# Spacing the search rounds of a routed expert layer by round, behind matmuls that set the clock

## The chip, the cores and the metric

One core of one Trainium2 chip runs the kernel. The metric is device microseconds from one execution, so smaller is better. TensorE is called PE below and its weight loads PEld; VectorE is DVE, ScalarE is ACT, GpSimd is POOL, and SP is the engine that issues most DMAs.

## The reference

Attention over 8 batches with 8 heads of 576 rows and 64 columns: half of the heads see a band of 32 keys, half see every 32nd key. Its output, as 4608 rows of 512, is routed to 8 experts of at most 576 rows each, and every expert is two matrix products with a ReLU between them. Rows are given out greedily over all scores in falling order:

```python
logits = x @ w_gate
order = np.argsort(-logits.flatten())
for idx in order:
    tok, e = idx // E, idx % E
    if assigned[tok] >= 0 or counts[e] >= cap:
        continue
    assigned[tok] = e
    counts[e] += 1
for e in range(E):
    mask = assigned == e
    out[mask] = np.maximum(x[mask] @ w1[e], 0.0) @ w2[e]
```

## The kernel before

**Two stages.** The attention stage fills some 236 us. It leaves the rows in DRAM (`x_scr`) and the scores `L` in SBUF. The expert stage follows, and the change touches it alone.

**Experts in the order in which they fill.** The kernel doesn't sort. It finds which expert is full first, and at which score; it gives that expert its rows, closes it, points the other rows to their next best expert, and searches for the next one to fill. The expert that fills first is phase 0, the last one is phase 7. Each phase runs one expert: a first layer (192 matmuls of 288 columns, L1167, in eight blocks of 24), then a second layer (96 of 512 columns, L1215, and 24 half-height ones, L1209). After each block of the first layer ACT writes the ReLU `hh` (L1174) and DVE the remainder `hl` (L1175), since every product is made from f16 halves.

**A search** (`search`) has seven rounds, 0 to 6. A round cuts an interval of scores in 18. DVE compares all rows with 17 candidates (`cm`, L811). PE counts (nine matmuls, L827), DVE folds the counts (`red` L830, `r` L833), PE sums them (L836), DVE compares them with the capacity (`g`, L843, or L840 in round 6), PE adds that up (L846), and DVE makes the next candidates (`cand`, L849). Then `settle` and `number` name the expert, `weights` starts its weight loads, `slots` (L899 on PE) numbers its rows, `indices` turns the numbers into a list of rows (L955 and L963 on PE, `idx` on DVE L967), and `tokens` gathers the rows on POOL (L1072, five gathers `xr`). `halve` splits them into f16 halves on ACT and DVE (`xg`, L1061 and L1062) and transposes them by DMA into `xt` (L1063). `xt` and the halved weights are what the next phase needs. The weights take squares on ACT (`jk`, L994), a scale (L1000, L1002 on PE, L208), and a halving on ACT (L1012) and DVE (L1013), sixteen pieces in all.

**What sets the order.** PE's order is the order in which the program is written out, and everything there waits in that order. `ffn` yields a cost after each matmul (123 for 288 columns, 216 for 512), and a clock in the program adds these up. Each chain of side work (search, list, weights) is a generator: it yields the number of units after which its next step is written out, and a step's matmuls land on PE at that point between the expert's own. So the yields of `search` are the spacing between a step's work on DVE and the matmul that consumes it, in units of about one ns of PE's own work. The other engines' order comes from the scheduler of the framework, which takes the steps by priority (`urgent`) and by its own estimate of times; on the chip each engine then works through its list in order. `side` runs the searches one behind the other, and the search for expert `ph` may not end before phase `ph - 2` is written out. Once phase `ph` begins, the steps of its weights that are left are written out at once (`rush`).

**What the steps of the prediction touch.** `pace` in `search` gives the units of a step: 2950 before the counts, 1350 before the sum, 1225 before the step (`T_COUNT`, `T_SUM`, `T_STEP`), and 0.55 of them while only one expert is closed, which is the search for expert 1. `T_HOT` (4200) stands between the comparisons of the list and L955, with `T_HOT1` (6350) for expert 1.

Of the kernel before, what the change touches and what calls it, by code (L numbers as in the profile page):

```python
# [19 lines left out]
N, DM, E, FF = B * S, H * D, 8, 1024  # L20
# [28 lines left out]
URGENT = 4000  # L49
T_FIRST, T_COUNT, T_SUM, T_STEP, T_PREFIX, T_NEXT, T_HOT, T_DUP, T_LOAD = 1100, 2950, 1350, 1225, 3900, 2300, 4200, 550, 8000  # L50
PACE1 = 0.55
H0 = 256
HURRY = (0, 1, 7)
MAN, MAN0, MANP = {mybir.EngineType.PE}, {mybir.EngineType.Activation}, (0,)
T_W20, T_STEP0 = 9000, 1000
X1 = 100
# [3 lines left out]
T_F, T_LOAD0, T_HOT1, T_W, T_SQ, T_SCALE, T_CUT, T_BULK0 = 3000, 1500, 6350, 4000, 1500, 1500, 1500, 600  # L60
# [77 lines left out]
def band_stride_attention_then_capacity_moe(ctx, tc, qt, kl, ks, nl, ns, wg, w1, w2, cst, out, dbg=None):  # L138
# [81 lines left out]
    with tc.tile_pool(name="ld", bufs=2) as ld, \  # L220
# [20 lines left out]
        for g in "sl":  # L241
            for i in range(2):
                t = ld.tile([128, 32], F32, name=f"mx_{g}{i}", bufs=1)
                nc.gpsimd.memset(t, 0.0)
                mxb[g, i] = t
                t = ld.tile([128, ST if g == "s" else LT, 4, VW], F32, name=f"v_{g}{i}", bufs=1)
# [481 lines left out]
    scat, closed, first, second = [], [], [], []  # L728
    ready, emitted, rush = set(), set(), set()

    def urgent(ph=1):
        return tc.high_priority(offset=URGENT * (2 if ph == 0 else 1))
# [12 lines left out]
    def settle(hp, top, w):  # L745
        mm = rt.tile([TP, 1], F32, name="mm")
        nc.vector.tensor_reduce(mm, hp, axis=AX.X, op=OP.max)
        w8 = rt.tile([TP, E], F32, name="w8")
        nc.vector.scalar_tensor_tensor(w8, hp, mm, desc8, op0=OP.is_equal, op1=OP.mult)
        mv = rt.tile([TP, 1], F32, name="mv")  # L750
        nc.vector.scalar_tensor_tensor(mv, mm, -1.0, w, op0=OP.add, op1=OP.mult)
        nc.vector.tensor_tensor(mv, mv, top, op=OP.add)
        return mv, w8
# [43 lines left out]
                    nc.tensor.matmul(pm[:, :E], ones_j[:J], g, start=True, stop=True)  # L797
                    return settle(pm[:, :E], top, grid[:, rd, J0:])

    def pace(t):  # L800
        return t if len(closed) > 1 else t * PACE1

    def search(rm, ohc, more):
        cand, src, top = cand0, rm, None
        ohv = ohc.rearrange("p c e -> p (c e)")
        for rd in range(R1):
            last = rd == R1 - 1
            t = cand[:, :J1] if last else cand[:, 1:J1 + 1]
            with urgent():
                cm = rt.tile([TP, NC, J1], F16, name="cm")  # L810
                nc.vector.tensor_tensor(cm, src[:, :, None].to_broadcast([TP, NC, J1]),  # L811
                                        t[:, None, :].to_broadcast([TP, NC, J1]), op=OP.is_ge)
                cv = cm.rearrange("p c j -> p (c j)")
                n = 1 if rd == R1 - 2 else J1 + 1
                if not last:
                    pre = cand[:, 0:1]
                    if n > 1:
                        pre = rt.tile([128, n], F32, name="pre1")
                        nc.vector.tensor_scalar(pre, steps[:, rd + 1, :n], cand[:, 0:1], None, op0=OP.add)
                if rd == 0:  # L820
                    more()
            yield pace(T_COUNT) + (X1 if len(closed) == 1 else T_FIRST if rd == 0 else 0)
            with urgent():
                pr = ps_r.tile([128, 512], F32, name="pr_")
                pc, p2, pm = pr[:GC * J1, :GC * E], pr[:, 64:64 + E], pr[:, 128:128 + (E if last else 1)]
                for k in range(0, NC, GC):
                    nc.tensor.matmul(pc, cv[:, k * J1:(k + GC) * J1], ohv[:, k * E:(k + GC) * E], start=(k == 0),  # L827
                                     stop=(k == NC - GC))
                red = rt.tile([GC * J1, GC, E], F16, name="red")
                nc.vector.tensor_tensor(red.rearrange("p c e -> p (c e)"), pc, fold[:, :GC * E], op=OP.mult)  # L830
                r8 = rt.tile([GC * J1, E], F16, name="r8")
                with nc.allow_low_precision(reason="whole numbers up to 1152"):
                    nc.vector.tensor_reduce(r8, red.rearrange("p c e -> p e c"), axis=AX.X, op=OP.add)  # L833
            yield pace(T_SUM)
            with urgent():
                nc.tensor.matmul(p2, fold[:, GC * E:], r8, start=True, stop=True, skip_group_check=True)  # L836
                g = rt.tile([128, E], F16, name="g1")
                ih = rt.tile([128, 1], F16, name="ih1")
                if last:
                    nc.vector.tensor_scalar(g, p2, float(CAP), None, op0=OP.is_ge)  # L840
                else:
                    with nc.allow_low_precision(reason="zero or one"):
                        nc.vector.tensor_scalar(g, p2, float(CAP), 0.0, op0=OP.is_ge, op1=OP.max, accum_out=ih)  # L843
            yield pace(T_STEP)
            with urgent():
                nc.tensor.matmul(pm, ones_j, g if last else ih, start=True, stop=True, skip_group_check=True)  # L846
                if not last:
                    cand = rt.tile([128, n], F32, name=f"cand{n}")
                    nc.vector.scalar_tensor_tensor(cand, steps[:, rd, J1 + 1:].to_broadcast([128, n]), pm, pre,  # L849
                                                   op0=OP.mult, op1=OP.add)  # L850
                if rd == R1 - 2:
                    top, src = cand, rt.tile([TP, NC], F32, name="rml")
                    nc.vector.tensor_scalar(src, rm, top, None, op0=OP.subtract)
                    cand = steps[:, rd + 1, :J1 + 1]
        with urgent():
            return settle(pm, top, steps[:, R1 - 1, J1 + 1:])
# [72 lines left out]
    def indices(ph, slot):  # L929
        hurry = ph in HURRY  # L930
        with urgent(ph) if hurry else nullcontext():
            si = rt.tile([TP, 2, NC], I32, name="si")
            nc.vector.tensor_copy(si[:, 0], slot)
            nc.vector.tensor_single_scalar(si[:, 1], si[:, 0], SLO - 1, op=OP.bitwise_and)
            nc.vector.tensor_single_scalar(si[:, 0], si[:, 0], 6, op=OP.logical_shift_right)
            sh = rt.tile([TP, 2, NC], F16, name="sh")
            nc.vector.tensor_copy(sh, si)
            ohh = rt.tile([TP, SHI, NC], F16, name="ohh")
            nc.vector.tensor_tensor(ohh, sh[:, 0:1].to_broadcast([TP, SHI, NC]), iota[:, :SHI], op=OP.is_equal)
            rv = rvb[ph % 2]  # L940
            nc.vector.tensor_tensor(rv[:, :3 * SHI].rearrange("p (h a) c -> p h a c", a=3), ohh[:, :, None].to_broadcast([TP, SHI, 3, NC]),
                                    val[:, None].to_broadcast([TP, SHI, 3, NC]), op=OP.mult)
            nh = NC // 3
            ohl = []
            for h in range(3):
                o = r1.tile([TP, SLO, nh], F16, name=f"ohl{h}")
                nc.vector.tensor_tensor(o, sh[:, 1:2, h * nh:h * nh + nh].to_broadcast([TP, SLO, nh]),
                                        iota[:, :, :nh], op=OP.is_equal)
                ohl.append(o)
        yield T_HOT1 if ph == 1 else T_HOT  # L950
        with urgent(ph):
            pi = ps_r.tile([128, 512], F32, name="pr_")
            for c in range(NC):
                g = c % 4
                nc.tensor.matmul(pi[HV * g:HV * g + HV, :SLO], rv[:, :, c], ohl[c // nh][:, :, c % nh], start=(c < 4),  # L955
                                 stop=(c >= NC - 4), skip_group_check=True)
            p1 = rt.tile([128, SLO], F16, name="p1")
            nc.vector.tensor_copy(p1, pi[:, :SLO])
        yield T_DUP
        with urgent(ph):  # L960
            p2 = ps_r.tile([128, 512], F32, name="pr_")
            for u in range(2):
                nc.tensor.matmul(p2[SLO * u:SLO * u + SLO, :2 * NT], p1, pick[:, u], start=True, stop=True,  # L963
                                 skip_group_check=True)
            idx = rt.tile([128, 2, NT], I32, name="idx", bufs=3)
            nc.vector.tensor_copy(idx.rearrange("p a t -> p (a t)"), p2[:, :2 * NT])
            nc.vector.tensor_single_scalar(idx[:, 1], idx[:, 1], 23, op=OP.logical_shift_left)  # L967
        return idx[:, 0], idx[:, 1].bitcast(F32)
# [208 lines left out]
    def ffn(ph, wts, xt, idx, sx):  # L1177
# [5 lines left out]
        if ph == 0:  # L1183
            t0 = H0 // 128
            for f in first[TURN_E:t0]:
                f()
            for c in (slice(0, H0), slice(H0, CAP)):
                for f in range(FC):
# [150 lines left out]
```

## Time and profile before

| | us |
|---|---|
| median of three runs | 696.55 |
| lowest, highest | 696.18, 700.16 |
| the profiled execution | 693.16 |
| its span, first to last instruction | 691.4 |
| PE busy in the span | 615.7 (89%) |
| DVE busy | 460.1 (67%) |
| ACT busy | 330.6 (48%) |
| POOL busy | 111.5 (16%) |
| mean granted clock of PE | 0.947 |

All times in the text are positions in the profiled execution's span, which ends 1.76 us short of that execution's time. In the rows, a bracket at the end is how long the engine had stood idle before that instruction, and what ended this. A busy PE means little here, since a matmul's duration overlaps the next one's; the distance from one start to the next, and the waits, say what a phase costs.

### The profile page before, as it was taken

To read this page: it belongs to the slowest core of one execution; us is meant where nothing else is said; L and a number is where in the kernel's file an instruction comes from. 1 tells how busy PE (TensorE), PEld (TensorE's weight loads), DVE (VectorE), ACT (ScalarE), POOL (GpSimd) and SP (SyncE) were. 2 spreads that over 40 slices of the span, in tenths; PEclk is the share of its full clock that TensorE was granted. 3 is DMA by queue.
4 is the path that set the end of the run, shared out by engine and by line. 5 is a ranking of instruction groups with operands and counts; after the bars stand their busy time and mean duration, and the time that the engine had idled before them with its cause. 6 is when DMAs were issued, how large, how long until landed. Compare 5 with 4: busy or idle time off the path is not lost.

```text
span 691.4 us, 19758 instructions
## 1 busy us (share of the span) xinstructions
PE 615.7 (89%) x8294; PEld 404.1 (58%) x8298; DVE 460.1 (67%) x1389; ACT 330.6 (48%) x551; POOL 111.5 (16%) x124
## 2 busy tenths in 40 slices
PE   8789998999964789989989979989999998999993
PEld 4567776766743465457448537547646744745741
DVE  4857776787857879786776777777778656580200
ACT  2443643464410644772762564484385277771210
POOL 2100110111000200410340140051042041211011
PEclk9898998999965899999999999999999998999997
DMA  8996888795210821860870770590293188731010
GB/s 233 250 256 176 249 234 212 212 265 162 68 41 2 271 65 35 306 109 1 298 153 1 264 172 16 177 241 33 105 270 78 60 276 236 221 59 50 1 39 31
DMA packets 76364, 102.42 MB, mean 148 GB/s; under 512 B 41292, under 2 KB 49062, under 8 KB 75763
## 3 DMA queue, kind: packets, MB, share of 16 engines
q1 hardware_dynamic: 68195, 79.61, 40.9%
q0 software_dynamic: 7360, 21.15, 9.9%
q8 instruction: 65, 1.06, 0.7%
q10 hardware_dynamic: 720, 0.39, 0.2%
q14 instruction: 24, 0.20, 0.1%
HBM read 73.60 MB, written 18.87 MB: 134 GB/s over the span
## 4 chain that ended last, share of the span: by engine, by line
PE 23%; issue 13%; DVE 10%; DMA 10%; POOL 4%; ACT 3%; SPq 1%; POOLq 0%; DVEq 0%; ACTq 0%
PE ph L1167 16%; DMA w<-in_w_dram 4%; DMA xr<-x_scr,idx 4%; PE ph L1215 3%; POOL xr L1072 3%; DVE w1l L1013 2%; DMA xt<-xg 2%; DVE w2l L1013 2%; POOL out_dram L1226 1%; DVE xg L1062 1%; DVE cm L811 1%; ACT jk L994 1%; PE ph L1209 1%; DVE hl L1175 1%; ACT xg L1061 1%
## 5 line engine op out<-in xcount | busy, mean ns | idle before, releaser
L1167 PE MATMUL ph<-xt,w1h 128*128 128x288 f16 (+2 forms) x1024 | 177.9, 289 | 6.4 <-DMA xt<-xg 4.1
L1167 PEld LDWEIGHTS <-w1h 128*128 128x128 f16 x1024 | 97.6, 99 | 37.8 <-issue 7.7
L1167 PE MATMUL ph<-xt,w1l 128*128 128x288 f16 (+2 forms) x512 | 111.7, 289 | 0.0
L1226 POOL DMA_INDIRECT out_dram<-y,idx x40 | 49.6, 1239 | 332.5 <-ACT y L1225 304.4
L1215 PE MATMUL ph<-w2h,hh 128*128 128x512 f16 x256 | 97.0, 379 | 0.8 <-DVE hl L1175 0.8
L1215 PE MATMUL ph<-w2h,hl 128*128 128x512 f16 x256 | 97.0, 379 | 0.0
L1215 PE MATMUL ph<-w2l,hh 128*128 128x512 f16 x256 | 97.0, 379 | 0.0
L994 ACT ACTIVATE jk<-w 128x1024 f16<-128x1024 f32 x64 | 67.4, 1054 | 61.6 <-DMA w<-in_w_dram 60.6
L1174 ACT ACTIVATE hh<-ph 128x576 f16<-128x576 f32 (+2 forms) x72 | 42.6, 593 | 110.8 <-PE ph L1167 110.6
L1215 PEld LDWEIGHTS <-hh 128*128 128x128 f16 x512 | 49.1, 98 | 58.2 <-issue 7.8
L1175 DVE SCALAR_TENSOR_TENSOR hl<-ph,hh 128x576 f16<-128x576 f32 (+2 forms) x72 | 49.5, 687 | 47.4 <-ACT hh L1174 47.3
L1167 PEld LDWEIGHTS <-w1l 128*128 128x128 f16 x512 | 50.5, 99 | 14.1 <-issue 1.3
L373 ACT ACTIVATE pr<-spa 128x576 f32<-128x576 f32 x32 | 20.8, 650 | 72.0 <-PE spa L370 50.3
L1072 POOL DMA_INDIRECT xr<-x_scr,idx x40 | 41.8, 1045 | 53.3 <-DVE L L920 25.3
L1013 DVE SCALAR_TENSOR_TENSOR w1l<-w,w_sw,w1h 128x512 f16<-128x512 f32 x64 | 45.5, 744 | 4.7 <-ACT w1h L1012 4.5
L1215 PEld LDWEIGHTS <-hl 128*128 128x128 f16 x256 | 24.9, 97 | 39.3 <-issue 14.3
L1013 DVE SCALAR_TENSOR_TENSOR w2l<-w,w_sw,w2h 128x512 f16<-128x512 f32 x64 | 46.4, 744 | 1.8 <-ACT w2h L1012 1.6
L1012 ACT ACTIVATE w2h<-w,w_sw 128x512 f16<-128x512 f32 x64 | 41.2, 710 | 6.0 <-DVE w_sw L208 6.0
L1012 ACT ACTIVATE w1h<-w,w_sw 128x512 f16<-128x512 f32 x64 | 42.4, 708 | 3.2 <-DVE w_sw L208 2.1
L1225 ACT ACTIVATE y<-ph,so 128x512 f32<-128x512 f32 x32 | 21.7, 679 | 43.9 <-PE ph L1215 31.6
L424 POOL DMA_DIRECT2D x_scr<-xs x23 | 15.3, 670 | 168.0 <-DVE xs L408 125.2
L1062 DVE TENSOR_TENSOR xg<-xr,xg 128x512 f16<-128x512 f32 (+1 forms) x37 | 25.3, 687 | 18.5 <-ACT xg L1061 18.3
(603 smaller groups left out, 951.5 us busy)
## 6 DMA issues: line engine op xcount, KB each, us to landing
w<-in_w_dram SPq DMA_DIRECT2D x64, 512.0 KB
kl<-in_kl_dram SPq DMA_DIRECT2D x16, 304.0 KB
v_s<-in_ns_dram SPq DMA_DIRECT2D x16, 292.5 KB
v_l<-in_nl_dram SPq DMA_DIRECT2D x16, 292.5 KB
ks<-in_ks_dram SPq DMA_DIRECT2D x16, 288.0 KB
qs<-in_qt_dram SPq DMA_DIRECT2D x16, 288.0 KB
ql<-in_qt_dram SPq DMA_DIRECT2D x16, 288.0 KB
x_scr<-xl SPq DMA_DIRECT2D x8, 512.0 KB
```

The costliest lines, as they stand in the source:

```text
L373: nc.scalar.activation(pr[:, :S].rearrange("k (h n) -> k h n", h=2), u.sp[p][:, :, :HS], AF.Exp, scale=0.125)
L994: nc.scalar.activation(jk, wf[:, c * n4:(c + 1) * n4].rearrange("p c f -> p (c f)"), AF.Square, scale=1.41422, accum_out=sq[:, c:c + 1])
L1012: nc.scalar.activation(hi[:, c, f], wf[:, c, f], AF.Copy, scale=s_)
L1013: nc.vector.scalar_tensor_tensor(lo[:, c, f], wf[:, c, f], s_, hi[:, c, f], op0=OP.mult, op1=OP.subtract)
L1062: nc.vector.tensor_tensor(xs[:, 1], xv, xs[:, 0], op=OP.subtract)
L1072: nc.gpsimd.indirect_dma_start(out=xr[:n], out_offset=None, in_=x_rows, in_offset=bass.IndirectOffsetOnAxis(ap=idx[:n, t:t + 1], axis=0))
L1167: nc.tensor.matmul(tile_[:, j, :w], wt[:, d, f * 128:(f + 1) * 128], xt[:, d // 2, xx, d % 2, c], start=(k == 0), stop=(k == 3 * DC - 1))
L1174: nc.scalar.activation(hv, src, AF.Relu)
L1175: nc.vector.scalar_tensor_tensor(lv, src, 0.0, hv, op0=OP.max, op1=OP.subtract)
L1215: nc.tensor.matmul(py, a[:, f, ts_], w[:, f], start=(k == 0), stop=(k == len(todo) - 1))
L1225: nc.scalar.activation(y, py, AF.Copy, scale=so[:, t:t + 1])
L1226: st = nc.gpsimd.indirect_dma_start(out=out_rows, out_offset=bass.IndirectOffsetOnAxis(ap=idx[:n, t:t + 1], axis=0), in_=y[:n], in_offset= ...
```

## The change

Three numbers. In the searches for experts 2 to 6 (two or more experts closed), rounds 4, 5 and 6 have all three distances cut to 0.72: 2124, 972 and 882 units. In rounds 1 and 2 the distance between the counts (L827) and the sum (L836) grows by 1000, from 1350 to 2350. In the list of the last expert, the distance before L955 grows from 4200 to 6350. No instruction is added or taken away. A search is written out over 3 x 1547 - 2000 = 2641 units fewer, and since the searches follow one another, each later one starts earlier within its phase. Lines behind 51 have a number higher by one in the kernel after.

```diff
+PACE, CROWDED, T_MORE = (1, 1, 1, 1, 0.72, 0.72, 0.72), (1, 2), 1000
...
-    def pace(t):
-        return t if len(closed) > 1 else t * PACE1
+    def pace(t, rd):
+        return t * PACE[rd] if len(closed) > 1 else t * PACE1
...
-            yield pace(T_COUNT) + (X1 if len(closed) == 1 else T_FIRST if rd == 0 else 0)
+            yield pace(T_COUNT, rd) + (X1 if len(closed) == 1 else T_FIRST if rd == 0 else 0)
...
-            yield pace(T_SUM)
+            yield pace(T_SUM, rd) + (T_MORE if len(closed) > 1 and rd in CROWDED else 0)
...
-            yield pace(T_STEP)
+            yield pace(T_STEP, rd)
...
-        yield T_HOT1 if ph == 1 else T_HOT
+        yield T_HOT1 if ph in (1, E - 1) else T_HOT
```

DVE in phase 3, round 1 of the search for expert 5. `pr__7439` (before) and `pr__7396` (after) are the same PSUM tile of counts, `xg` are the halves of expert 4's gathered rows, `y` is output of the running phase. Before:

```order
L1062 TENSOR_TENSOR xg<-xr,xg 128x2x256
L830 TENSOR_TENSOR red<-pr__7439,fold 68x32
L1062 TENSOR_TENSOR xg<-xr,xg 128x2x256
L833 TENSOR_REDUCE r_7451<-red 68x8
L1062 TENSOR_TENSOR xg<-xr,xg 128x2x256
L843 TENSOR_SCALAR g_7467,ih_7468<-pr__7439 128x8
L1062 TENSOR_TENSOR xg<-xr,xg 128x2x256
```

After:

```order
L1063 TENSOR_TENSOR xg<-xr,xg 128x2x256
L831 TENSOR_TENSOR red<-pr__7396,fold 68x32
L1063 TENSOR_TENSOR xg<-xr,xg 128x2x256
L834 TENSOR_REDUCE r_7408<-red 68x8
L1063 TENSOR_TENSOR xg<-xr,xg 128x2x256
L1224 SCALAR_TENSOR_TENSOR y<-ph,so,yl 64x512
L1063 TENSOR_TENSOR xg<-xr,xg 128x2x256
L844 TENSOR_SCALAR g_7437,ih_7438<-pr__7396 128x8
```

The fourth `xg` and the output piece `y` have moved ahead of `g`, which PE's L846 (L847 after) consumes; the fold `r` stands behind two `xg` as it did.

PE in phase 5, the second part of the list for expert 6 (`p` and `pick` belong to the list, `w1l` to the first layer, `w2l`, `w2h`, `hh` and `hl` to the second). Before:

```order
L1215 MATMUL ph<-w2l,hh 128x512
L963 LDWEIGHTS p_8889
L963 MATMUL pr__8903<-pick,p_8889 64x10
L963 LDWEIGHTS p_8889
L963 MATMUL pr__8903<-pick,p_8889 64x10
L1215 LDWEIGHTS hl
L1215 MATMUL ph<-w2h,hl 128x512
```

After:

```order
L1168 MATMUL ph<-xt,w1l 128x288
L964 LDWEIGHTS p_8806
L964 MATMUL pr__8813<-pick,p_8806 64x10
L964 LDWEIGHTS p_8806
L964 MATMUL pr__8813<-pick,p_8806 64x10
L1168 LDWEIGHTS w1l
L1168 MATMUL ph<-xt,w1l 128x288
```

The list has moved from the second layer (behind 59 of its 120 matmuls) into the first layer (behind 185 of 192).

ACT in phase 5, around the end of the first layer: `jk` are squares of expert 6's weights, which wait for their loads. Before:

```order
L1174 ACTIVATE hh<-ph 128x576 x7
L994 ACTIVATE jk,sq<-w_8684 128x1024 x2
L1225 ACTIVATE y<-ph,so 128x512
L994 ACTIVATE jk,sq<-w_8684 128x1024 x2
L1222 ACTIVATE yl<-ph,so 64x512
```

After:

```order
L1175 ACTIVATE hh<-ph 128x576 x5
L995 ACTIVATE jk,sq<-w_8583 128x1024 x2
L1175 ACTIVATE hh<-ph 128x576
L995 ACTIVATE jk,sq<-w_8583 128x1024 x2
L1175 ACTIVATE hh<-ph 128x576
L995 ACTIVATE jk,sq<-w_8592 128x1024 x3
L1175 ACTIVATE hh<-ph 128x576
```

The squares now stand between the `hh` of the first layer, where they stood behind all of them.

## Prediction

> **What bounds the kernel now.** I read the table of stretches first, one stretch per phase of the expert stage. Its columns are busy time by engine (with counts), then the granted clock and the DMA share.
>
> ```profile
> 357.70:413.70 56.00, 51.96 (x433) 32.99 (x432) 40.94 (x128) 30.12 (x50) 12.36 (x10) 1.00 0.48 139
> 404.60:409.00 4.40, 4.18 (x22) 1.94 (x22) 3.72 (x12) 4.08 (x8) 0.00 (x0) 1.00 1.15 229
> 523.30:575.30 52.00, 50.79 (x401) 31.90 (x399) 35.22 (x118) 28.84 (x49) 9.13 (x10) 1.00 0.47 144
> 575.30:578.50 3.20, 0.26 (x1) 0.04 (x1) 2.91 (x9) 2.33 (x4) 1.58 (x2) 0.86 0.62 149
> 578.50:584.70 6.20, 6.16 (x27) 3.95 (x28) 3.40 (x5) 3.02 (x6) 0.00 (x0) 0.52 0.98 367
> 632.90:680.10 47.20, 47.20 (x313) 29.29 (x311) 6.80 (x9) 8.63 (x13) 4.78 (x5) 1.00 0.07 26
> ```
>
> The bare phase 7 takes 47.2 us at full clock: that is what PE needs for one expert. Phase 2 takes 56.0. So PE bounds the stage, and what can be won is PE's waits and its slow clock. Second, the list of PE's waits in this stage (total, times, longest):
>
> ```profile
> PE ph L1167 <- DMA xt<-xg: 4.1, 2, 3.0
> PE pr__6674 L836 <- DVE r L833: 2.8, 1, 2.8
> PE pr__7519 L836 <- DVE r L833: 1.8, 1, 1.8
> PE pr__5989 L836 <- DVE r L833: 1.7, 1, 1.7
> PE pr__9204 L955 <- DVE rv L941: 1.4, 1, 1.4
> PE pr__8284 L836 <- DVE r L833: 1.3, 1, 1.3
> PE pr__6754 L836 <- DVE r L833: 1.0, 1, 1.0
> PE pr__8204 L836 <- DVE r L833: 0.9, 1, 0.9
> PE pr__5142 L836 <- DVE r L833: 0.8, 1, 0.8
> PE pr__8903 L963 <- DVE p L958: 0.7, 1, 0.7
> PE pr__5909 L836 <- DVE r L833: 0.6, 1, 0.6
> PE pr__7439 L836 <- DVE r L833: 0.5, 1, 0.5
> PE pr__7628 L836 <- DVE r L833: 0.3, 1, 0.3
> ```
>
> The tiles 5909, 6674, 7439 and 8204 are round 1 of the searches for experts 3 to 6, and 5989, 6754, 7519 and 8284 their round 2. So the added 1000 units stand where PE waits most. Round 1 sums to 0.6 + 2.8 + 0.5 + 0.9 = 4.8 us, round 2 to 1.7 + 1.0 + 1.8 + 1.3 = 5.8.
>
> **Rounds 1 and 2, the first edit.** One such wait in phase 2, on DVE and in order:
>
> ```profile
> 396.03 0.17 DVE L967 TENSOR_SCALAR idx<-idx 128x5 int32<-128x5 int32 x1
> 401.84 0.18 DVE L830 TENSOR_TENSOR red<-pr__6674,fold 68x32 f16<-68x32 f32 x1
> 403.96 0.69 DVE L1062 TENSOR_TENSOR xg<-xr,xg 128x512 f16<-128x512 f32 x1 [1.93 <-ACT xg L1061]
> 404.57 0.20 DVE L833 TENSOR_REDUCE r<-red 68x8 f16<-68x32 f16 x1
> 406.13 0.69 DVE L1062 TENSOR_TENSOR xg<-xr,xg 128x512 f16<-128x512 f32 x1 [0.68 <-ACT xg L1061]
> ```
>
> DVE isn't short of time: it stands 1.93 us before the second `xg`, whose gathered rows aren't there yet, and the fold `r` (0.20 us) is queued behind it. 1000 units become four matmuls of 512 columns, 4 x 0.216 = 0.86 us. But the gathers start from `idx`, and the whole search moves with the list, so their distance to round 1 stays, and the new order puts up to four `xg` ahead of `g`. From phase 4:
>
> ```profile
> 507.19 0.17 DVE L967 TENSOR_SCALAR idx<-idx 128x5 int32<-128x5 int32 x1
> 513.81 0.20 DVE L833 TENSOR_REDUCE r<-red 68x8 f16<-68x32 f16 x1
> 515.71 0.69 DVE L1062 TENSOR_TENSOR xg<-xr,xg 128x512 f16<-128x512 f32 x1 [0.62 <-ACT xg L1061]
> ```
>
> PE reached that L836 at 514.0 - 0.9 = 513.1, 5.9 after `idx`; now it gets there at 6.8, and at L846 six matmuls (1.3 us) later, at 8.1. The fourth `xg` ends 515.71 + 0.69 - 507.19 = 9.2 after `idx` here, 10.8 in phase 2. With `g` behind it, PE waits 1.1 to 2.7 at L846 instead. By the order, `g` stands behind the fourth `xg` in three searches (in the first of them behind a weight piece too) and behind the third in the search for expert 4. I take 1.9, 0.3, 1.3 and 0.5 = 4.0, and 0.8 left at L836: as much as the 4.8 before. **Round 1 comes to 0**, bounded by a gain of 4.8 if the gathers land sooner and a loss of some 6 if each is as late as in phase 2 (4 x 2.7 - 4.8). In round 2, the last `xg` and most weight pieces now stand ahead of `cm`, and the four extra matmuls come on top: I leave 0.9 of 5.8, **-4.9**, between -5.8 and -3.4 (0.86 won at each of four, less than that nowhere). The 0.8 of tile 5142 is in phase 0. What it wins is waited for again at phase 1's first matmuls, where 4.1 - 3.0 = 1.1 us go to `xt`, whose gathers and transposes don't move: 0.
>
> **Rounds 4 to 6, the second edit.** Round 6 in phase 2, in the first layer:
>
> ```profile
> 378.49 0.45 PE L827 MATMUL pr__6324<-ohn,cm 128*68 128x32 f16 x9
> 379.19 0.20 DVE L833 TENSOR_REDUCE r<-red 68x8 f16<-68x32 f16 x1
> 380.13 0.17 PE L836 MATMUL pr__6324<-r,fold 68*128 68x8 f16 x1
> 380.36 0.17 DVE L840 TENSOR_SCALAR g<-pr__6324 128x8 f16<-128x8 f32 x1 [0.97 <-PE pr__6324 L836]
> 381.16 0.76 DVE L1175 SCALAR_TENSOR_TENSOR hl<-ph,hh 128x576 f16<-128x576 f32 x1 [0.63 <-ACT hh L1174]
> 381.38 0.17 PE L846 MATMUL pr__6324<-g,ones_j 128*128 128x8 f16 x1
> ```
>
> `r` is ready 0.74 us before its matmul (380.13 - 379.39) and `g` 0.85 (381.38 - 380.53). The cut takes away three and two matmuls of 0.123, so 0.37 and 0.60 are left. In itself the second edit is free; nothing is cheaper either, since no work goes. An `hl` in between (0.76) now costs up to 0.4 at `r`. More costly is where rounds 3 and 4 come to lie: at a phase's start, among the second weight's pieces.
>
> ```profile
> L1013 DVE SCALAR_TENSOR_TENSOR w2l<-w,w_sw,w2h 128x512 f16<-128x512 f32 x64 | 46.4, 744 | 1.8 <-ACT w2h L1012 1.6
> ```
>
> One piece of 0.744 us between `red` and `r` exceeds the 0.37 by 0.4. Round 3 already paid 0.3 there (tile 7628). For four searches, two rounds, one such piece each I take 8 x 0.4 - 3 x 0.3 = **+2.3**, between 0 and +5.
>
> **What the drift moves.** The searches get 2641 units shorter, so by phase 5 the list for expert 6 is written out 7 matmuls of 0.123, 24 + 11 of 0.216 and 24 of 0.109 sooner: 0.9 + 7.6 + 2.6 = 11 us. At the start of phase 6 stands the largest stall of the stage:
>
> ```profile
> 561.89 0.17 DVE L967 TENSOR_SCALAR idx<-idx 128x5 int32<-128x5 int32 x1
> 578.54 0.90 PE L1167 MATMUL ph<-xt,w1h 128*128 128x288 f16 x3 [2.98 <-DMA xt<-xg]
> 597.85 1.06 ACT L994 ACTIVATE jk<-w 128x1024 f16<-128x1024 f32 x1 [2.78 <-DMA w<-in_w_dram]
> 600.19 0.63 ACT L1174 ACTIVATE hh<-ph 128x576 f16<-128x576 f32 x1
> ```
>
> `xt` was complete 16.7 us after its `idx` (578.54 - 561.89), 3 us too late; 11 us sooner, it is there 8 us early. That saves the 2.98, and the half clock behind it: 6.20 us at 0.52 is a loss of 6.20 x 0.48 = 2.98. **-6.0**, at least -3 should the clock fall elsewhere. On the clock, the 2.8 us wait of phase 2 left it at 1.00 (404.60 to 409.00), the 3.2 us stretch brought it to 0.52. [...]
>
> The list itself now lies in the first layer in phases 4 and 5 (and at its end in phase 3). There its steps on DVE share the queue with `hl`, which waits for `hh`, which on ACT now stands behind squares that wait for weight loads, as in phase 6 before: a square stood 2.78 us, and the `hh` behind it came at 600.19. PE has three PSUM buffers in `ph`, which covers a late `hh`; what isn't covered is L955 and L963 of the list. I take one `hl` (0.76) in phases 4 and 5, half in phase 3, less the 0.7 of tile 8903: **+1.2**, between -0.7 and +6 (two squares' waits of 2.78).
>
> **The last list, the third edit.** 2150 units are 17 matmuls, 2.1 us, against 1.4 of tile 9204; but ACT and DVE begin phase 6 with expert 7's squares ahead of second-weight pieces, and its `slots` step behind an `hl`. **-0.7**, between -1.4 and +0.7.
>
> Sum: 0 - 4.9 + 2.3 - 6.0 + 1.2 - 0.7 = -8.1. The profiled execution took 693.16, so 685.1. The median of the runs shown is 3.4 higher, at 696.55, and I forecast for that: **688.5**, or -1.2%.
>
> **Rivals.** *The wait moves* (no change): `g` and round 3 take back what `r` gives, so that only the phase 6 term and some of round 2 are left, -6.0 - 3.4 + 5 + 1.2 = -3.2, or 693. For it speaks that the gathers set the end of round 1. *The half clock at round 1* (slower): `g` waits behind the fourth `xg` until the stall passes 3 us. From there each costs some 3 idle and, as in phase 6, 3 of slow clock; in three searches 3 x 6 = 18, less the 4.8 paid before, is +13, and with the rest (-8.1) +5; with two rounds 3 hit alike +12: 702 to 708, 705. Against it: the fourth `xg` ended 9.2 and 10.8 after `idx`, so waits of 1.1 to 2.7, under 3. *All waits go* (much faster): gathers that no scatter precedes land sooner, -4.8 - 5.8 - 6.0 - 0.7 - 1.4 = -18.7, and round 3 is free: 678. Against it speaks the order of `xg` and `g`.
>
> **How the numbers follow.** Forecast 0.45 (684 to 692), the wait moves 0.29, all waits go 0.14, half clock 0.12. About 1% is what a measurement of this kernel tells from no change: 689.6 to 703.5. Faster holds all of the third and four fifths of the forecast, 0.50; within 1% the rest and the moved wait, 0.38; slower 0.12. A range of 680 to 698 leaves out the half clock and the edge of the best case.
>
> **What would show it.** Right: no wait for `xt` at phase 6 and a clock of 1.00 there; round 2's L836 under 0.5 each; new waits at round 1's L846 on `g`, 1 to 2 us. Wrong: a stretch at 0.5 of the clock in phases 1 to 5; waits at L955 or L963 of over 2 us; round 1 without any wait; phase 6 still over 50 us.

## The result, and the profile after

The median is 700.36 us over 21 runs, against 693.34 for the kernel before over 21 runs beside them: a ratio of 1.0097 (95% interval 1.0071 to 1.0123). A later set gave the same kernel 1.0052 (1.0017 to 1.0088). The change makes it 0.5 to 1% slower. The forecast was 688.5, from 696.55, the median of the three runs known then.

The two profiled executions hide this (693.16 before, 693.24 after, which is the fastest of its 21 runs): the attention stage, which the change doesn't touch, took 236.9 us in the one and 230.5 in the other, up to the first L1167 (L1168 after). The expert stage alone went from 443.2 to 449.7, +6.5. By phase, from the first matmul of one to the first of the next:

| phase | 0 | 1 | 2 | 3 | 4 | 5 | 6 | 7 |
|---|---|---|---|---|---|---|---|---|
| before, us | 64.4 | 56.4 | 56.0 | 55.2 | 54.4 | 52.0 | 57.6 | 47.2 |
| after, us | 63.7 | 60.8 | 59.1 | 55.1 | 59.0 | 51.2 | 53.5 | 47.2 |

Phase 6 won 4.1; phases 1, 2 and 4 lost 12.1. The table of stretches of the kernel after (columns as before: PE, PEld, DVE, ACT and POOL busy, granted clock, DMA share, GB/s), phase 6 and then two stretches behind a stall, in phases 1 and 4:

```profile
579.50:633.00 53.50, 49.62 (x356) 30.37 (x355) 31.56 (x66) 31.64 (x53) 11.01 (x11) 1.00 0.42 112
345.20:350.20 5.00, 4.98 (x23) 2.09 (x23) 4.36 (x9) 3.69 (x8) 0.76 (x1) 0.66 0.61 138
511.70:517.70 6.00, 6.00 (x29) 2.58 (x29) 5.40 (x12) 3.89 (x8) 2.03 (x1) 0.72 0.78 174
```

Phase 6 runs at full clock now. The slow clock has moved to phases 1 and 4: a loss of 5.0 x 0.34 + 6.0 x 0.28 = 3.4 us. The list of PE's waits shows what stands ahead of these stretches:

```profile
PE pr__5893 L847 <- DVE g L844: 4.4, 1, 4.4
PE pr__8141 L847 <- DVE g L844: 2.6, 1, 2.6
PE pr__6738 L828 <- DVE cm L812: 2.1, 1, 2.1
PE ph L1168 <- DMA xt<-xg: 1.9, 2, 1.0
PE pr__6648 L837 <- DVE r L834: 1.9, 1, 1.9
PE pr__7653 L837 <- DVE r L834: 1.6, 1, 1.6
PE ph L1168 <- DVE hl L1176: 1.5, 1, 1.5
PE pr__7396 L847 <- DVE g L844: 1.2, 1, 1.2
PE pr__8080 L964 <- DVE p L959: 1.1, 1, 1.1
PE pr__9228 L956 <- DVE rv L942: 1.0, 1, 1.0
PE pr__6738 L837 <- DVE r L834: 1.0, 1, 1.0
```

5893, 6648, 7396 and 8141 are round 1 of the four searches; 6738 is round 2 of the second. Round 1 waits 4.4 + 1.9 + 1.2 + 2.6 = 10.1 us, where before it waited 4.8. The longest of these, in phase 1, on DVE in order:

```profile
332.63 0.17 DVE L968 TENSOR_SCALAR idx<-idx 128x5 int32<-128x5 int32 x1
338.33 0.69 DVE L1063 TENSOR_TENSOR xg<-xr,xg 128x512 f16<-128x512 f32 x1 [0.54 <-ACT xg L1062]
338.94 0.20 DVE L834 TENSOR_REDUCE r<-red 68x8 f16<-68x32 f16 x1
342.07 0.69 DVE L1063 TENSOR_TENSOR xg<-xr,xg 128x512 f16<-128x512 f32 x1 [2.93 <-ACT xg L1062]
343.73 0.69 DVE L1063 TENSOR_TENSOR xg<-xr,xg 128x512 f16<-128x512 f32 x1 [0.96 <-ACT xg L1062]
344.33 0.74 DVE L1014 SCALAR_TENSOR_TENSOR w1l<-w,w_sw,w1h 128x512 f16<-128x512 f32 x1
345.00 0.15 DVE L844 TENSOR_SCALAR_CACHE_REDUCE g<-pr__5893 128x8 f16<-128x8 f32 x1
```

`g` (0.15 us) stands behind two `xg` and a weight piece; DVE itself stands idle 2.93 us for the third row tile. The fourth `xg` ends 343.73 + 0.69 - 332.63 = 11.8 after `idx`. In phases 1 to 4 it came 9.9, 10.8, 9.5 and 9.2 us after `idx` in the kernel before, and 11.8, 13.7, 9.5 and 11.0 in the kernel after. POOL's queue says why, in phase 1 (three rows) and in phase 2 (two rows, whose `idx` came at 389.37):

```profile
334.15 0.96 POOL L1073 DMA_INDIRECT xr<-x_scr,idx  x1 [0.30 <-issue]
335.42 3.11 POOL L1073 DMA_INDIRECT xr<-x_scr,idx  x1 [0.30 <-issue]
338.83 1.02 POOL L1073 DMA_INDIRECT xr<-x_scr,idx  x1 [0.30 <-issue]
...
390.87 0.97 POOL L1227 DMA_INDIRECT out_dram<-y,idx  x1 [33.70 <-ACT y L1226]
392.14 0.98 POOL L1073 DMA_INDIRECT xr<-x_scr,idx  x1 [0.30 <-issue]
```

In phase 1 the third gather held POOL for 3.11 us instead of 0.96. In phase 2 a scatter (L1227), which waited for ACT's `y`, stands ahead of the gathers, so the first one starts 2.8 us after `idx` instead of 0.24.

### The profile page after: what moved, and what is told of

Read it like the earlier page. It is cut to its first block, busy times and chain, and to the rows that moved or that the text cites. A ratio compares the mean times of both kernels' runs of the same rounds, so it can differ in the third digit from the quotient of the medians.

```text
span 691.5 us, 19754 instructions
## 1 busy us (share of the span) xinstructions
PE 615.1 (89%) x8294; PEld 402.4 (58%) x8298; DVE 460.9 (67%) x1389; ACT 330.4 (48%) x551; POOL 109.1 (16%) x124
## 4 chain that ended last, share of the span: by engine, by line
issue 20%; PE 17%; DVE 9%; DMA 9%; POOL 5%; ACT 4%; SPq 1%; POOLq 0%; DVEq 0%; ACTq 0%
PE ph L1168 9%; PE ph L1216 6%; DMA w<-in_w_dram 5%; POOL xr L1073 3%; DVE w2l L1014 3%; DMA xr<-x_scr,idx 3%; POOL out_dram L1227 2%; ACT jk L995 2%; DVE w1l L1014 1%; DVE cm L812 1%; ACT hh L1175 1%; ACT w2h L1013 1%; SPq L980 1%; DVE hl L1176 1%; ACT xg L1062 1%
## 5 line engine op out<-in xcount | busy, mean ns | idle before, releaser
L1168 PE MATMUL ph<-xt,w1h 128*128 128x288 f16 (+2 forms) x1024 | 175.8, 287 | 6.4 <-DMA xt<-xg 1.9
L1168 PEld LDWEIGHTS <-w1h 128*128 128x128 f16 x1024 | 97.3, 98 | 37.1 <-issue 8.8
L1168 PE MATMUL ph<-xt,w1l 128*128 128x288 f16 (+2 forms) x512 | 111.3, 287 | 0.0
L1216 PE MATMUL ph<-w2h,hh 128*128 128x512 f16 x256 | 98.5, 385 | 0.0
L1216 PE MATMUL ph<-w2h,hl 128*128 128x512 f16 x256 | 98.4, 384 | 0.0
L1227 POOL DMA_INDIRECT out_dram<-y,idx x40 | 44.6, 1115 | 264.7 <-ACT y L1226 244.7
L1073 POOL DMA_INDIRECT xr<-x_scr,idx x40 | 44.6, 1114 | 129.9 <-DVE idx L968 94.5
L1168 PEld LDWEIGHTS <-w1l 128*128 128x128 f16 x512 | 49.2, 98 | 16.4 <-issue 4.9
L1226 ACT ACTIVATE y<-ph,so 128x512 f32<-128x512 f32 x32 | 21.8, 681 | 47.2 <-PE ph L1216 37.5
```

The source lines that it names most:

```text
L1073: nc.gpsimd.indirect_dma_start(out=xr[:n], out_offset=None, in_=x_rows, in_offset=bass.IndirectOffsetOnAxis(ap=idx[:n, t:t + 1], axis=0))
L1168: nc.tensor.matmul(tile_[:, j, :w], wt[:, d, f * 128:(f + 1) * 128], xt[:, d // 2, xx, d % 2, c], start=(k == 0), stop=(k == 3 * DC - 1))
L1216: nc.tensor.matmul(py, a[:, f, ts_], w[:, f], start=(k == 0), stop=(k == len(todo) - 1))
L1226: nc.scalar.activation(y, py, AF.Copy, scale=so[:, t:t + 1])
L1227: st = nc.gpsimd.indirect_dma_start(out=out_rows, out_offset=bass.IndirectOffsetOnAxis(ap=idx[:n, t:t + 1], axis=0), in_=y[:n], in_offset= ...
```

## The experiments

Theory one, "`g` behind `xg`": the added units only move PE's wait from `r` to `g`, which stands behind later row tiles. Theory two, "drift": the added units are harmless, the earlier lists do the damage. In the traces "phases 1 to 4" are 222.0 us before and 234.1 after. The kernel with the third edit alone (below), whose instructions are those of before up to phase 5, has 225.9, so one trace is good to some 4 us.

**Added units without drift.**

```diff
-PACE, CROWDED, T_MORE = (1, 1, 1, 1, 0.72, 0.72, 0.72), (1, 2), 1000
+PACE, CROWDED, T_MORE = (1, 1, 1, 1, 0.8793, 0.8793, 0.8793), (1, 2), 1000
```

(and `T_HOT` for the last list, as before)

> The added 1000 units in rounds 1 and 2, with rounds 4 to 6 shortened by the same 2000 units (factor 0.8793), so that the lists stay where they were; last list as before. Theory 'g behind xg': PE's wait only moves from r to g and passes 2.5 us in two or three searches, the clock falls behind it, so phases 1 to 4 together are some 12 us longer than before's 222.0, phase 6 keeps its stall for xt: ratio to before about 1.015. Rival 'drift': without the earlier lists the gathers come as in before, the waits at L846 are 1 to 2 us, phases 1 to 4 within 2 us of 222: ratio 1.000.

Ratio 1.0052 (1.0015 to 1.0090), phases 1 to 4 at 225.5. Its waits, and the stretches behind those of 6675 and 7440:

```profile
PE pr__5910 L847 <- DVE g L844: 2.6, 1, 2.6
PE pr__6675 L847 <- DVE g L844: 2.2, 1, 2.2
PE pr__8205 L847 <- DVE g L844: 2.2, 1, 2.2
PE pr__7440 L847 <- DVE g L844: 2.2, 1, 2.2
...
406.90:412.90 6.00, 5.87 (x28) 2.49 (x28) 4.87 (x13) 3.30 (x6) 1.64 (x1) 0.72 0.95 177
463.30:469.30 6.00, 5.79 (x38) 2.75 (x38) 4.90 (x14) 3.36 (x7) 1.65 (x1) 1.00 0.74 185
```

All four searches now wait at `g` in round 1, 9.2 us in all, and no longer at `r` in rounds 1 and 2, where they waited 10.6. The wait has moved, as theory one says, and most of it is still there. What the added units won is lost elsewhere: round 3 now waits 4.2 us (0.9 before), and two of the four stalls at `g` have a slow clock behind them, 1.7 us each. Of the three equal waits one has the clock at 0.72 behind it, the others have it at 1.00. The loss is smaller than theory one's number, but the drift isn't needed for it.

**The drift alone.**

```diff
+PACE, CROWDED, T_MORE = (1, 1, 1, 1, 0.8407, 0.8407, 0.8407), (1, 2), 0
```

> The drift alone: no added units in rounds 1 and 2, rounds 4 to 6 shortened by 2641 units (factor 0.8407) per search, as far as the whole change shortens a search; last list as before. Theory 'g behind xg': phases 1 to 4 as before (222, waits at L836 as before), phase 6 without the stall for xt at 53 to 54 instead of 57.6: ratio 0.993. Rival 'drift': gathers behind scatters and late xg, phases 1 to 4 at 230 as in after, phase 6 at 53.5: ratio 1.010.

Ratio 1.0025 (0.9978 to 1.0072): neither number. In its trace phases 1 to 4 took 228.5, nearer to the 230 of the rival than to 222, with 6.6 us of waits in round 1 (4.8 before). Phase 6 did lose its stall for `xt` (57.6 to 54.8), but other waits took its place:

```profile
PE pr__9206 L956 <- DVE rv L942: 4.3, 1, 4.3
PE pr__8833 L964 <- DVE p L959: 2.4, 1, 2.4
```

The first belongs to the last list, which lies in the first layer of phase 6 as it did before; its comparisons on DVE stand behind `ss` and an `hl`, which wait for ACT among the squares. The second belongs to the list of phase 5, which now lies right behind the first layer. So the drift gains at phase 6 and gives it back, at the lists and perhaps in phases 1 to 4.

**The last list alone.**

```diff
+PACE, CROWDED, T_MORE = (1, 1, 1, 1, 1, 1, 1), (1, 2), 0
+        yield T_HOT1 if ph in (1, E - 1) else T_HOT
```

> The third edit alone: the last list 2150 units later before L955. Both theories: the wait of 1.4 us at L955 for rv in phase 6 goes or becomes under 0.5, nothing else changes, 0 to -1.4 us: ratio 0.998 to 1.000. If it came to more than 1.002, slots behind an hl.

Ratio 0.9978 (0.9926 to 1.0031); the wait for `rv` is gone from its list of waits. As expected, and too small to be told from nothing.

**The searches start later.** `T_FIRST` from 1100 to 3741, rounds 4 to 6 at 0.72, nothing added.

> Round 0 starts 2641 units later (T_FIRST 3741), rounds 4 to 6 at 0.72, no added units in rounds 1 and 2, last list as before: rounds 0 to 3 lie 2.3 us later after the gathers, a search is 2000 units shorter. Theory 'g behind xg': r and g of round 1 come after nearly all xg, so waits at L836 and L846 in rounds 1 and 2 sum to under 5 us in phases 1 to 4 (10.6 before), phase 6 loses most of the xt stall: 8 us less, ratio 0.988. Rival 'drift': the earlier lists put gathers behind scatters, phases 1 to 4 at 225 or more: ratio 1.00 to 1.01.

Ratio 1.0116 (1.0042 to 1.0190). Theory one's forecast fell. In its trace PE waited 5.8 us for `r` in round 1 of phase 1, and in POOL's queue there a scatter now stands between the second gather and the third, which starts 4.5 us after `idx` instead of 2.8. A round that is moved away from the gathers is of no use where the gathers move too.

**Round 2 alone.** `CROWDED = (2,)`, rounds 4 to 6 at 0.9396; then with rounds 3 to 6 of the last search at 0.75, and the last list as in the change.

> The added 1000 units in round 2 alone, rounds 4 to 6 shortened by as much (factor 0.9396), last list as before: no drift. Theory 'g behind xg': round 1 waits as before (4.8), the waits of round 2 (5.8) sink to under 2, none at L846: phases 1 to 4 some 4 us shorter than in the kernel with both rounds and no drift (225.5): ratio 0.994 to 0.998. Rival 'drift': round 2 doesn't matter, ratio 1.000 to 1.003.

> As the kernel with 1000 units in round 2 alone, and in the search for expert 6 alone rounds 3 to 6 at 0.75, 5.5 - 0.4 = some 4 to 5 us earlier list for phase 6; last list 2150 units later as in the change. Theory 'g behind xg' with the drift paying in phase 6 alone: phase 6 at 53 to 54 without the wait for xt, phase 5 as before, -4 beside the former kernel: ratio 0.990 to 0.993. Rival 'drift': the list in phase 5 then waits at L963 for 2 to 3 us: ratio 0.998.

Ratios 0.9991 (0.9913 to 1.0069) and 1.0037 (0.9991 to 1.0082). In the first, round 2 still waits 1.6 + 1.8 + 0.9 = 4.3 us, and the waits for `xt` are 9.1 us (4.1 before). In the second the list of phase 6 waits 3.1 us for `rv`.

**The remainders `xg` on POOL.** In `halve`:

```diff
-            nc.vector.tensor_tensor(xs[:, 1], xv, xs[:, 0], op=OP.subtract)
+            nc.gpsimd.tensor_tensor(xs[:, 1], xv, xs[:, 0], op=OP.subtract)
```

> The whole change, and the remainders of the gathered rows (xg, five per expert) are worked out on POOL instead of DVE, so that r, g and cm can't stand behind them. Theory 'g behind xg': the waits at L847 for g (4.4 and 2.6 us) and L828 for cm (2.1) go, none over 1.0 is left in rounds 1 and 2, phases 1 to 4 are 222 or less instead of 234.1: ratio 0.985 to before. Rival 'drift': what is late is ACT, the weight pieces and the list, phases 1 to 4 stay above 230: ratio 1.005 or more. Open: xt comes later, since POOL is slower than DVE; a wait for xt at the start of phases 2 to 7 would show it.

> The kernel before, with xg on POOL in the same way. Theory 'g behind xg': the waits for r in rounds 1 and 2 (10.6 us in all) go to under 3, phases 1 to 4 at 214 to 216 instead of 222; phase 6 keeps its stall for xt or has a longer one: ratio 0.988 to 0.995. Rival 'drift': r waits for other work (c, cand), the waits stay at 6 or more: ratio 0.998 to 1.005.

Ratios 1.0283 (1.0213 to 1.0354) and 1.0311 (1.0240 to 1.0383). These don't tell the theories apart, since the edit makes a stall of its own. One row of POOL and one of DVE from the second kernel:

```profile
353.10 4.48 POOL L1063 TENSOR_TENSOR xg<-xr,xg 128x512 f16<-128x512 f32 x4
...
353.25 4.88 DVE L1014 SCALAR_TENSOR_TENSOR w1l<-w,w_sw,w1h 128x512 f16<-128x512 f32 x1 [3.06 <-ACT w1h L1013]
```

A weight piece, 0.74 us elsewhere, took 4.88 while POOL ran four subtractions, after 3.06 us of waiting for ACT's half of the piece, and `g` stood behind it: PE waited 5.7 to 6.4 us in each of the four searches. The median subtraction took 1.16 us on POOL in these two kernels, where it takes 0.69 on DVE.

**`g` ahead of the third `xg`.** DVE writes a one behind round 1's `g`, and the later remainders use it, so that they must follow:

```diff
+            if rd == 1 and len(closed) > 1:
...
+                    nc.vector.tensor_scalar(one, g[:, 0:1], 0.0, 1.0, op0=OP.mult, op1=OP.add)
...
+            if t >= 2 and ones_after:
+                nc.vector.scalar_tensor_tensor(xs[:, 1], xv, ones_after[-1][:n, 0:1], xs[:, 0], op0=OP.mult, op1=OP.subtract)
```

This was put into the kernel after, into the kernel before, and into the kernel without drift (there with the last list as in the change).

> The whole change, and the remainders xg of the third to fifth row tile are made to depend on a one (128x1) that DVE writes right after g of round 1, so that on DVE g no longer stands behind the third and fourth xg; the values stay the same. Theory 'g behind xg': the waits at round 1's g (4.4, 2.6, 1.2 us) sink to 1 or less, no stretch of slow clock behind them, phases 1 to 4 at 224 to 227 instead of 234.1: ratio 0.992 to 1.000. Rival 'drift' (late lists' gathers, weight pieces and y among the rounds): the waits go to r of round 1 or to cm and r of round 2, phases 1 to 4 stay above 230: ratio 1.006 or more.

> The kernel before with g ahead of the third xg in the same way. Here PE waited for r, which stands behind the second xg and stays there: both theories expect round 1 as before (4.8 us) and the waits of round 2 for r (5.8 us) as before or up to 2 us more, since the fourth and fifth xg come later: ratio 1.000 to 1.004.

> 1000 units more in rounds 1 and 2, rounds 4 to 6 shortened by as much (0.8793), g of round 1 ahead of the third xg, last list as in the change. Theory 'g behind xg': of the four waits of 2.2 to 2.6 us for g under 0.5 each is left, no slow clock behind them, phases 1 to 4 at 216 to 219 instead of 225.5, and last list 0 to -1: ratio 0.988 to 0.993, faster than both kernels. Rival: the wait comes back at round 2 (cm or r behind the fourth and fifth xg, 2 us each), phases 1 to 4 at 222 to 226: ratio 0.998 to 1.005.

Ratios 1.0122 (1.0067 to 1.0178), 0.9978 (0.9939 to 1.0016) and 0.9998 (0.9959 to 1.0036). In the first the waits went to round 2's `cm` (3.1 and 2.6) while one at `g` stayed (2.1). In the second they went to the phases' starts: 10.3 us for `xt` instead of 4.1. The third is the telling one: `g` still kept PE waiting 2.8, 2.1, 2.1 and 1.2 us, with no third or fourth `xg` ahead of it. Here is why, two rows of ACT and two of DVE:

```profile
462.51 0.63 ACT L1068 ACTIVATE xg<-xr 128x512 f16<-128x512 f32 x1 [1.11 <-DMA xr<-x_scr,idx]
463.05 1.04 ACT L1001 ACTIVATE jk<-w 128x1024 f16<-128x1024 f32 x1
...
464.22 0.16 DVE L1007 TENSOR_REDUCE ss<-sq 128x1 bf16<-128x4 f32 x1 [2.76 <-ACT jk L1001]
464.29 0.16 DVE L845 TENSOR_SCALAR_CACHE_REDUCE g<-pr__7446 128x8 f16<-128x8 f32 x1
```

`g` stands behind `ss`, `ss` waits for ACT's last square, and that square stands on ACT behind the copy of the fourth row tile, which waits for the fourth gather. Another queue leads to the same gather.

**`ss` behind the one as well.**

```diff
+                if ones_after and bits == W2_BITS:
+                    s1 = rt.tile([128, 4], F32, name="sq1")
+                    nc.vector.tensor_scalar(s1, sq, ones_after[-1], None, op0=OP.mult)
+                    sq = s1
```

> As the kernel without drift and with g ahead of the third xg, and now also ss (the sum of the weights' squares, which waits for ACT's squares, which stand on ACT behind the fourth xg) depends on the one written after g. Theory 'in-order queues behind the gathers': only now nothing ahead of g hangs on the fourth gather; the waits of 2.8, 2.1, 2.1, 1.2 us for g go to under 0.6 each, no slow clock behind them, phases 1 to 4 at 219 to 222 instead of 227.1 (the waits for xt stay): ratio 0.990 to 0.997. Rival 'PE has simply too little cover': the wait comes back at round 2 for cm or r with about the same sum, phases 1 to 4 at 225 to 228: ratio 0.998 to 1.004.

Ratio 1.0012 (0.9970 to 1.0053), phases 1 to 4 at 227.9 (227.2 without this edit). Only one wait for `g` of any size is left, but round 2 has the rest:

```profile
PE pr__8313 L829 <- DVE cm L813: 3.7, 1, 3.7
PE pr__6006 L829 <- DVE cm L813: 2.6, 1, 2.6
PE pr__7452 L853 <- DVE g L845: 1.4, 1, 1.4
...
523.75 0.74 DVE L1074 SCALAR_TENSOR_TENSOR xg<-xr,one,xg 64x512 f16<-64x512 f32 x1 [3.52 <-ACT xg L1072]
524.42 0.78 DVE L813 TENSOR_TENSOR cm<-rmn,cand 128x612 f16<-128x612 f32 x1
```

The rival holds: in the last of the four searches `cm` of round 2 stands behind the fifth `xg`. Each step freed from the gathers leaves the next one behind them.

**Lists moved once, and the two smallest edits together.** The first paced search alone is shorter by 2650 units (0.16 off its factors in rounds 4 to 6): on the kernel just shown, and on the kernel before with `g` ahead (both with the last list as in the change). Then `g` ahead and the last list alone.

> As the kernel before this, and the first of the four searches alone shorter by another 2650 units (rounds 4 to 6 at 0.72), so that all later lists and gathers come once 2.3 to 2.6 us earlier without moving on from phase to phase. Theory 'in-order queues behind the gathers': the waits for xt at the starts of phases 2 to 6 (some 7 us) go to under 2.5, the rest as in the kernel before this: ratio 0.983 to 0.990, faster than both kernels. Rival 'drift': the shifted lists meet scatters and ph's last blocks again, phases 1 to 4 at 228 or more: ratio 1.000 or more.

> The kernel before with g of round 1 ahead of the third xg, rounds 4 to 6 of the first of the four searches at 0.84 (2650 units earlier, once), last list as in the change; no units added anywhere. Theory 'in-order queues behind the gathers': the waits for xt (10.3 us) sink to under 4, r and g of round 1 wait as before (under 5 in all): ratio 0.985 to 0.992. Rival 'drift': new waits at r and cm behind scatters and weight pieces, ratio 0.998 or more.

> The two edits that came out at 0.998 each, together: the kernel before with g of round 1 ahead of the third xg, and the last list 2150 units later; nothing else. If their gains add: 0.993 to 0.997. If they were chance: 0.998 to 1.002. Waits: none over 1.5 us at g or r, those for xt stay at some 10 us (2 to 3 each at the starts of phases 1, 2, 5 and 6), the 1.6 us for rv goes.

Ratios 1.0030 (0.9983 to 1.0077), 1.0045 (1.0007 to 1.0083) and 0.9981 (0.9949 to 1.0012). In the second the waits for `xt` did fall, to 2.1 us, and `r` and `cm` took 2.5 and 2.5 in their stead. Nothing here is shown to be faster than the kernel before.

**The changed kernel once more.**

> The changed kernel once more, for a second trace of it: which of its waits come again and which hang on one execution. Both theories: ratio 1.005 to 1.012. Theory 'in-order queues behind the gathers': the waits at round 1's g in phases 1 and 4 (4.4 and 2.6 us) and at round 2's cm in phase 2 (2.1) come again within 1.5 us, phases 1 to 4 at 230 to 238, since the order that causes them is fixed. Rival 'chance': the stretched gather (3.1 us) was one bad draw, without it phase 1 has a wait under 2, phases 1 to 4 at 225 to 228.

Ratio 1.0052 (1.0017 to 1.0088), phases 1 to 4 at 238.5, the expert stage at 453.4 (449.7 in the first trace). Its waits, and its third gather of phase 1:

```profile
PE pr__5893 L847 <- DVE g L844: 6.3, 1, 6.3
PE pr__7396 L847 <- DVE g L844: 2.6, 1, 2.6
PE pr__8141 L847 <- DVE g L844: 2.5, 1, 2.5
PE pr__6738 L828 <- DVE cm L812: 1.9, 1, 1.9
...
343.38 3.10 POOL L1073 DMA_INDIRECT xr<-x_scr,idx  x1 [0.30 <-issue]
```

The waits stand at the same steps and the third gather is stretched again, 3.10 us. The places are fixed by the order; the sizes vary by some 2 us. Of 7396's 2.6 us (1.2 in the first trace) 1.1 are a pause of DVE ahead of `g` whose cause the trace doesn't name.

## Why the prediction was wrong

By its own terms, from the two traces:

| term | predicted | measured | from |
|---|---|---|---|
| round 1 | 0 | +8.7 | waits 4.8 to 10.1, slow clock 3.4 |
| round 2 | -4.9 | -2.7 | 5.8 to 2.1 + 1.0 |
| rounds 3 and 4 | +2.3 | +3.7 | 3 x 0.3 to 1.6 + 0.9 + 0.8 + 0.8 + 0.3 + 0.2 |
| start of phase 6 and last list | -6.7 | -4.1 | phase 6, 57.6 to 53.5 |
| lists in the first layer | +1.2 | +1.4 | 0.7 to 1.1 + 0.3 + 0.3 + 0.2 + 0.2 |
| sum | -8.1 | +7.0 | the stage itself: +6.5 |

That the sum comes so near to the stage is in part luck: 1.4 us of waits won in phase 0 and 0.7 lost at the start of phase 1 stand in no term.

**Round 1 failed, and it decides.** That `g` would stand behind late `xg` was right, and so was the direction: the wait moves from `r` to `g`. Two steps of its size were wrong. First, "the gathers start from `idx`, and the whole search moves with the list, so their distance to round 1 stays". The distance in units stayed, but not that in time. The prediction had 1.9, 0.3, 1.3 and 0.5 us for the four searches and measured were 4.4 at `g`, 1.9 at `r`, 1.2 and 2.6 at `g`. In the third, whose fourth `xg` came as before (9.5), it is right to 0.1; in the first and the last the fourth `xg` came 1.9 and 1.8 us later than before, and the wait is 2.5 and 2.1 longer than forecast; in the second all five came late. POOL took its list in order: in phase 2 the drift put a scatter ahead of the gathers, and the first of them started 2.8 us after `idx` (0.24 in the kernel before), and in phase 1 the third gather held POOL for 3.11 us, in the second trace for 3.10. I had costed SP's and DVE's queues and not POOL's. What stretches that gather isn't shown. Second, waits "under 3" were to leave the clock alone, an estimate that lay between two rows (2.8 us with the clock at 1.00 behind it, 3.2 us with 0.52), but it fell behind 2.6 us in phase 4, and in the kernel without drift behind 2.2 us in one of three cases. Together the two make the +8.7, over the bound of +6.

The kernel without drift shows that late gathers aren't needed for a loss. PE reached L847 8.2 us after `idx` there, as the prediction said (8.1), and the fourth `xg` ended 9.6 to 10.0 after it, within 9.2 to 10.8; but DVE's order is another in that kernel, `g` stands behind the fourth `xg` and a weight piece in all four searches, and it began at 10.1 to 10.6. The 9.2 us of waits there are within the bound too.

Of the rivals "the half clock at round 1", to which I gave 0.12, comes nearest: two stalls of round 1 have a slow clock behind them, at 4.4 and 2.6 us. It asked for three, and 700.36 lies under its 702 to 708.

**Round 2** was won by half: in phase 2 it waits again, at `cm`, behind the fourth `xg` (which starts at 402.42 in that trace, 13.05 after `idx`). **Rounds 3 and 4** were mis-sized by 1.4, within their bound. **The lists'** sum held, but not their place: the list stands in the first layer in phase 5 alone (behind 180 and 185 of its 192 matmuls), and behind all 192 in phases 3 and 4. **Phase 6** runs without the wait for `xt` and at a clock of 1.00, as said; but waits for `hl` (1.5, 0.8 before) and `y` (0.9), which I hadn't named, took part of it back, and its 53.5 us stay above the 50 that the prediction named as a sign against it. The last list won nothing: its wait at L956 fell from 1.4 to 1.0, and a new one at its L964 (tile 9274) took 0.5.

How the loss divides between added units and drift is not settled to better than the intervals allow: 1.0052, 1.0025 and 0.9978 for the three parts alone make 1.0055 together, which is the second measurement of the whole and half of the first.

## What to carry to other kernels

A wait at the head of an in-order queue isn't removed by giving its consumer more time, if what it waits for comes later than the next steps too: here it went from `r` (10.6 us in rounds 1 and 2) to `g` (9.2), from there to `cm` (3.7 and 2.6, with `ss` behind the one as well), and in the kernel before with `g` ahead to `xt` (10.3 instead of 4.1). Follow the wait through every queue to the transfer at its root, and ask first whether that can come sooner; no run here made the gathers come sooner, so what that would win isn't shown. When a whole chain is moved, check the queues that it doesn't own (here POOL's scatters): what stood ahead of the first transfer decided, 2.8 us instead of 0.24, not the distance in the plan.

## What the hardware showed that I had not expected

**The clock falls behind stalls of 2 us already, and their place decides.** In 16 traces I took the stalls of PE of 1 us or more in phases 1 to 6 that had none other over 0.5 us in the 4 us before them, and looked at the granted clock in the 6 us behind each. Below 2.0 us it had fallen in 7 of 58, from 2.0 to 2.5 in 10 of 20, from 2.5 to 3.1 in 9 of 13, above in 12 of 12, in most cases to 0.72, which costs 6 x 0.28 = 1.7 us. It looks like chance, but the traces show more. In each of them the granted clock is 1.00 or 0.50, and it changes only on a grid of 3.41 us. In phases 1 to 6 of the trace before it was at 0.50 from 577.59 to 584.42, two windows of 3.41, and the stretch at 1.00 ahead of them lasts 334.51 us, 98 windows; in the trace after it was at 0.50 from 345.57 to 348.98 and from 512.82 to 516.24, one window each. The grid lies elsewhere from one execution to the next: its boundaries are 0.7 us past a multiple of 3.413 in the trace before, 0.8 in the one after and 2.0 in that of the kernel without drift. In phases 0 to 6 of these traces I took every window of the grid that was at full clock itself. Where PE stood idle for over 2.0 us of it, the next window was at 0.50 in 44 of 44 cases; from 1.6 to 2.0 us in 17 of 40, from 1.2 to 1.6 in 2 of 73, below that in 0 of 1639. Two of the equal stalls in the kernel without drift, those of 6675 and 7440, each with its window and the next:

```profile
404.80:408.21 3.41, 1.24 (x8) 0.58 (x7) 2.79 (x8) 3.31 (x6) 0.00 (x0) 1.00 1.25 261
408.21:411.62 3.41, 3.41 (x10) 1.21 (x9) 3.31 (x7) 2.02 (x4) 1.64 (x1) 0.50 1.06 172
459.41:462.82 3.41, 1.82 (x10) 0.71 (x8) 1.87 (x5) 2.24 (x6) 1.15 (x2) 1.00 1.05 236
462.82:466.23 3.41, 2.85 (x15) 1.29 (x14) 3.10 (x9) 3.11 (x7) 0.34 (x1) 1.00 1.16 252
```

The first stall lies whole in one window (3.41 - 1.24 = 2.17 us idle) and the next window is at half clock; the second is cut by the grid into 1.59 and 0.56, and the clock stays. So it was with the prediction's two rows: the grid cut the 2.8 us of phase 2 into 1.5 and 1.3, while in the window ahead of the slow clock of phase 6 PE stood idle for 2.4. Since the grid lies elsewhere from one execution to the next, the price of a stall in this kernel is better taken as an expected value that grows with its length than as a limit.

**DVE beside subtractions on POOL was slower.** The 4.88 us weight piece above ended at 358.13, 0.55 us after the last of the four subtractions. It is one of 21 DVE instructions with two inputs that took 1.6 to 5.1 us in the two kernels with `xg` on POOL, all of them beside a subtraction on POOL; in the other 16 traces none took over 0.96. Less clear is the stretched indirect DMA: in all 18 traces 25 of 1350 on POOL in the expert stage took over 2 us, up to 5.03, and 23 of them were scatters. DVE's instructions with two inputs filled 0.59 to 0.98 of each; but they also filled over 0.85 of 166 others, which took under 1.1 us, so they alone don't explain it, and this was not tried by itself.
